# Gated linear attention on one core: the decayed state joins the new k v in PSUM, and VectorE decays it from there

## The chip, the cores and the metric

The kernel runs on one core of a Trainium2 chip. The metric is the device time of one execution in microseconds (us), the median of several; lower is better. The engines are PE (TensorE), DVE (VectorE), ACT (ScalarE), POOL (GpSimd) and SP, whose queue issues most DMAs.

## The reference

Attention with a decaying state, then a soft mixture of experts, then an ELU layer. The change touches the first part alone.

```python
B, H, S, D = 4, 8, 768, 48
state = zeros(B, H, D, D)
for t in range(S):
    state = alpha[:, :, t, :, None] * state + einsum('bhd,bhe->bhde', k[:, :, t], v[:, :, t])
    y[:, :, t] = einsum('bhd,bhde->bhe', q[:, :, t], state)
x = y as (B*S, H*D)
# soft MoE: logits = x @ phi, softmax over tokens and over slots, 8 experts, relu
# then elu(x @ w_in) @ w_out
```

## The kernel before

**Units and chunks.** Tokens come in 24 units of 128 (4 batches of 6), each of two chunks of 64 (g = 0, 1). A tile has the 48 channels of a head in each half of its partitions (h2 = 0, 1, at rows 0 and 64), and four such pairs (j) side by side. Within a chunk the work is matrix products; from chunk to chunk a state of 48 x 48 per head is carried.

**One unit.** `d_sfx` (L421) scans alpha backwards into `sfx`, whose column 0 is the decay over a whole chunk; `d_k` (L426) multiplies k by it in place in the `ring` buffer. `d_ini` (L429, GpSimd) clamps that decay from below; `d_pr` takes its reciprocal (L433) and scans alpha forwards into `pr` (L435). `d_q` (L449) multiplies q by it into `r`, and `d_q2` copies half of `r` (ScalarE, shown as L296, the line of the helper `copy`). `pe_a` (L472) makes the products of k and q, `a_evac` (L478) copies them out, and `mask` (L485, two GpSimd selects) writes their triangle into the other half of `r`. `pe_ktr` (L460) transposes k; `v_move` copies v to other rows. `pe_kv` (L514) makes k v of both chunks in PSUM, in two banks `kv_ps[0]` and `kv_ps[1]`. `pe_y` (L557) multiplies `r` by a tile `vsr` that holds v and, below it, the state, so that one product gives both parts of y; ScalarE copies y to `x`.

**The state.** For each chunk `s_add` (L527, VectorE) adds the decayed state `sp` to k v from PSUM into `sn`; `s_mul` (L537, GpSimd, by `ENG`) multiplies `sn` by the next chunk's decay into `sp`; `s_put` copies `sp` into `vsr` (ScalarE, two copies). At a batch's last chunk nothing is added, and the state in `vsr` is set to zero.

**The order.** `STEP` is an order written by hand: at step s each name is run for unit s - lag, so ("sfx", -2) works on unit s + 2. Steps run from -2 to 23. Each engine takes its instructions in this order. Alongside, one piece of `w_in` per step, in float64, is split into a high and a low part: `conv_a` (L84, L86, L93 on VectorE, L92 on ScalarE) and, a step later, `conv_b` (L659, GpSimd); `loads` fetches the next piece and a part of the expert weights. Every fourth step has work on a group of four units (`post_a`, `post_b`, `post_c`: L579 to L620). The rest of the expert weights is loaded once the attention's buffers are free.

```python
STEP = [("busy0", 0), ("cb", 0), ("kv", 0), ("vc", -1), ("pb", 3), ("sfx", -2), ("ini", -2), ("add0", 0), ("mul0", 0),
        ("busy2", 0), ("a", -1), ("put0", 0), ("k", -2), ("lqka", -1), ("add1", 0), ("mul1", 0), ("pr", -2),
        ("ev", -1), ("put1", 0), ("busy3", 0), ("q", -2), ("ca", 0), ("q2", -2), ("pc", 4), ("loads", 0),
        ("mask", -1), ("pa", 2), ("xtr", 1), ("y", 0), ("check", -2), ("busy1", 0), ("ktr", -2), ("lv", 0)]
```

Of the kernel before, what the change touches and what calls it, by code (L numbers as in the profile page):

```python
# [10 lines left out]
F32 = mybir.dt.float32  # L11
# [43 lines left out]
WPART = 3  # L55
BUSY = (4, 0, 0, 0)

STEP = [("busy0", 0), ("cb", 0), ("kv", 0), ("vc", -1), ("pb", 3), ("sfx", -2), ("ini", -2), ("add0", 0), ("mul0", 0),
# [217 lines left out]
def gla_softmoe_elu_kernel(ctx, tc, qka, vs, vt, phi, w1, w2, w_in, w_out, out):  # L276
    nc = tc.nc
    ctx.enter_context(tc.manual_schedule())
    V, A_, G, T, SY = nc.vector, nc.scalar, nc.gpsimd, nc.tensor, nc.sync
# [122 lines left out]
    st = {}  # L402
# [22 lines left out]
    def d_k(u):  # L425
        eng["k"][0].tensor_mul(split(ks(u)), split(ks(u)), st[u]["sfx"][:, :, 1:])  # L426

    def d_ini(u):
        G.tensor_scalar_max(ini[:, :, 0:1], st[u]["sfx"][:, :, 0:1], DLOW)  # L429

    def d_pr(u):
        a = ring[u % RING][:, 2 * QC:]
        V.reciprocal(ini[:, :, 0:1], ini[:, :, 0:1])  # L433
        pr = wd.tile([128, NP * 2, AW], F32, tag="pr", name="pr")
        V.tensor_tensor_scan(out=flat(pr), data0=a[:, 0:ACOL], data1=flat(ini),  # L435
                             initial=0.0, op0=ALU.mult, op1=ALU.add)
        st[u]["pr"] = pr
# [78 lines left out]

    sp = [None]

    def s_add(u, g):
        if last(u, g):  # L520
            return
        if u % NC == 0 and g == 0:
            sn = wk.tile([128, NP, D], F32, tag="sn", name="sn")
            V.tensor_copy(sn, kv_ps[g])
        else:
            sn = wk.tile([128, NP, D], F32, tag="sn", name="sn")
# [12 lines left out]
    def s_put(u, g):
        if last(u, g):  # L540
# [603 lines left out]
```

## Time and profile before

| | us |
|---|---|
| median of 3 runs | 347.75 (347.74 to 349.73) |
| the profiled execution, its time | 349.67 |
| its span | 347.9 |
| busy: PE, DVE, ACT, POOL | 292.7, 256.1, 206.5, 197.7 |
| steps of the attention, by starts of `pr` | 20.74 to 174.32, 21 steps |

Times in rows are us from the start of the span. A row of a timeline gives the start, the length, the engine, the line, the operation, output and input tiles, shapes, how many instructions are merged, and in brackets how long the engine had been idle and what ended that. Lengths of neighbours on one engine can overlap a little, so what a step costs an engine is read from start to start.

### The profile page before, as it was taken

How to read it: one execution, taken by the hardware profiler on the slowest of the kernel's cores; microseconds unless marked ns; L12 is line 12 of the kernel's file. 1: busy time of each engine (PE TensorE's matmuls, PEld its weight loads, DVE VectorE, ACT ScalarE, POOL GpSimd, SP SyncE). 2: the span in 40 equal slices, each digit the busy share in tenths (PEclk: the TensorE clock that was granted, in tenths of full speed). 3: DMA queues.
4: the chain of work that ended last, by engine and by line, in shares of the span. 5: the costliest groups of instructions: out<-in, count | busy, mean ns of one | idle time of the engine just before them, and what ended most of it. 6: DMA issues, size and time to landing. Idle time of an engine off the chain costs nothing.

```text
span 347.9 us, 9142 instructions
## 1 busy us (share of the span) xinstructions
PE 292.7 (84%) x3632; PEld 214.4 (62%) x3632; DVE 256.1 (74%) x491; ACT 206.5 (59%) x440; POOL 197.7 (57%) x266
## 2 busy tenths in 40 slices
PE   8768688776787676977779899989989999999992
PEld 3766566655566555765656455457767777578881
DVE  5988899998999989999871456189986776176650
ACT  1456676866777677687576223259867657164541
POOL 5476777577577676757753012004689888255450
PEclk9969878999898999699889899999999999999998
DMA  7646887687777777767556889991000000002442
GB/s 287 183 140 218 275 266 255 206 245 260 236 282 210 250 246 253 268 220 219 181 192 259 343 313 424 416 423 61 1 2 0 0 3 0 0 2 110 179 168 96
DMA packets 22049, 66.88 MB, mean 192 GB/s; under 512 B 2416, under 2 KB 8560, under 8 KB 20976
## 3 DMA queue, kind: packets, MB, share of 16 engines
q1 hardware_dynamic: 21296, 63.86, 52.2%
q10 hardware_dynamic: 704, 2.37, 1.8%
q8 instruction: 31, 0.51, 0.6%
q14 instruction: 18, 0.15, 0.1%
HBM read 61.50 MB, written 4.72 MB: 190 GB/s over the span
## 4 chain that ended last, share of the span: by engine, by line
PE 37%; DVE 28%; POOL 15%; ACT 8%; DMA 7%; issue 3%; ACTq 0%; DVEq 0%; SPq 0%; POOLq 0%
PE z_ps L1024 14%; DVE pr L435 8%; POOL wl L659 6%; DMA wo<-w_out 5%; PE hf_ps L996 5%; DVE r L449 4%; PE y_ps L557 4%; POOL ini L429 4%; POOL sp L537 3%; DVE sfx L421 3%; DVE rr L1008 2%; PE h_ps L845 2%; DMA ring<-qka 2%; PE kt_ps L460 2%; DVE sn L527 2%
## 5 line engine op out<-in xcount | busy, mean ns | idle before, releaser
L1024 PE MATMUL z_ps<-rr,wor 128*128 128x512 f32 x288 | 75.8, 395 | 0.8 <-POOL rr L1009 0.8
L557 PE MATMUL y_ps<-vsr,r 128*64 128x64 f32 x768 | 43.8, 250 | 27.3 <-ACT vsr L296 26.6
L1024 PEld LDWEIGHTS z_ps<-rr,wor 128*128 128x128 f32 x288 | 53.5, 188 | 15.4 <-POOL rr L1009 3.4
L1009 POOL TENSOR_TENSOR rr<-mm 128x512 fp32r<-128x512 f32 x36 | 38.6, 1077 | 33.6 <-ACT mm L1002 33.6
L557 PEld LDWEIGHTS y_ps<-vsr,r 128*64 128x64 f32 x768 | 34.5, 156 | 37.4 <-ACT vsr L296 32.5
L485 POOL TENSOR_SCALAR_AFFINE_SELECT r<-at 64x512 f32<-64x512 f32 x48 | 46.5, 969 | 17.4 <-ACT at L478 15.8
L296 ACT COPY vsr<-sp 48x192 f32<-48x192 f32 x88 | 30.8, 350 | 30.7 <-POOL sp L537 29.3
L1002 ACT ACTIVATE mm<-hf_ps 128x1024 f32<-128x1024 f32 x36 | 36.8, 1027 | 15.6 <-PE hf_ps L996 12.5
L659 POOL TENSOR_TENSOR wl<-cva,cvb 128x256 bf16<-128x256 f32 x24 | 30.9, 1289 | 18.5 <-ACT x L296 10.7
L472 PE MATMUL at_ps<-r,ring 64*64 64x64 f32 x768 | 35.3, 235 | 4.5 <-ACT r L296 2.9
L435 DVE TENSOR_TENSOR_SCAN pr<-ring,ini 128x520 f32<-128x520 f32 x24 | 35.7, 1486 | 0.8
L472 PEld LDWEIGHTS at_ps<-r,ring 64*64 64x64 f32 x768 | 30.6, 148 | 7.9 <-ACT r L296 4.7
L1008 DVE SCALAR_TENSOR_TENSOR rr<-hf_ps,mm 128x512 fp32r<-128x512 f32 x36 | 24.8, 688 | 13.3 <-ACT mm L1002 13.0
L996 PE MATMUL hf_ps<-cst,gst 128*128 128x512 f32 x96 | 31.4, 409 | 1.7 <-ACT gst L1078 0.7
L421 DVE TENSOR_TENSOR_SCAN sfx<-ring,imp 128x520 f32<-128x520 f32 x24 | 30.2, 1260 | 2.3 <-DMA ring<-qka 2.3
L537 POOL TENSOR_TENSOR sp<-sn,sfx 128x192 f32<-128x192 f32 x44 | 24.7, 562 | 10.0 <-DVE sn L527 9.9
L296 ACT COPY r<-r 64x512 f32<-64x512 f32 x24 | 14.8, 616 | 19.9 <-DVE r L449 19.6
L527 DVE TENSOR_TENSOR sn<-kv_ps,sp 128x192 f32<-128x192 f32 x40 | 13.8, 346 | 14.4 <-POOL sp L537 11.0
L449 DVE TENSOR_TENSOR r<-ring,pr 128x512 f32<-128x512 f32 x24 | 20.7, 861 | 2.3
L996 PEld LDWEIGHTS hf_ps<-cst,gst 128*128 128x128 f32 x96 | 17.0, 188 | 8.3 <-DVE rr L1008 2.0
L815 POOL COPY c<-chi 128x128 f32<-128x128 f32 x12 | 3.9, 354 | 29.7 <-DVE chi L812 29.7
L429 POOL TENSOR_SCALAR ini<-sfx 128x8 f32<-128x8 f32 x24 | 13.8, 573 | 12.3 <-DVE sfx L421 12.3
(179 smaller groups left out, 596.5 us busy)
## 6 DMA issues: line engine op xcount, KB each, us to landing
ring<-qka SPq DMA_DIRECT2D x22, 772.5 KB, 5.7
w<-w SPq DMA_DIRECT2D x8, 1536.0 KB, 9.7
w<-w SPq DMA_DIRECT2D x21, 512.0 KB, 5.1
raw<-w_in SPq DMA_DIRECT2D x24, 256.0 KB, 2.7
wo<-w_out SPq DMA_DIRECT2D x8, 768.0 KB, 15.5
vsr<-vs SPq DMA_DIRECT2D x48, 96.0 KB, 4.8
out<-wi SPq DMA_DIRECT2D x4, 768.0 KB, 4.0
ring<-qka ACTq DMA_DIRECT2D x2, 772.5 KB, 7.6
```

The costliest lines, as they stand in the source:

```text
L296: (e.copy if e is A_ else e.tensor_copy)(out, in_)
L421: V.tensor_tensor_scan(out=flat(sfx)[:, ::-1], data0=a[:, 1:ACOL + 1][:, ::-1], data1=flat(imp)[:, ::-1], initial=0.0, op0=ALU.mult, op1=A ...
L435: V.tensor_tensor_scan(out=flat(pr), data0=a[:, 0:ACOL], data1=flat(ini), initial=0.0, op0=ALU.mult, op1=ALU.add)
L472: T.matmul(out=at_ps[64 - p0:128 - p0, j, t0:t0 + C], lhsT=k[p0:p0 + 64, j, t0:t0 + C], rhs=r[p0:p0 + 64, h2, j, t0:t0 + C], start=True, s ...
L485: G.affine_select(out=split(r[p0:p0 + 64, h2]), in_=split(at[p0:p0 + 64]), pattern=[[0, 2 * NP], [1, C]], compare_op=ALU.is_ge, fill=0.0, ...
L537: eng[f"mul{g}"][0].tensor_mul(sp[0], sn, pe.to_broadcast([128, NP, D]))
L557: T.matmul(out=y_ps[t0:t0 + C, 2 * j + h2, :], lhsT=r[:, h2, j, t0:t0 + C], rhs=vsr[u % RING][:, h2, g, D * j:D * j + YW], start=True, sto ...
L659: at(s, 2, lambda i: eng["f64b"][0].tensor_mul(wi_lo(i), cva, cvb.bitcast(F32)))
L996: T.matmul(out=h_ps[:, x, :], lhsT=gst[:, 128 * f:128 * f + 128], rhs=cst[:, TG * grp:TG * grp + TG], start=True, stop=True)
L1002: A_.activation(m, hp[p], AF.Relu, scale=-1.0)
L1009: G.tensor_mul(r[1], m[:, 1], m[:, 1])
L1024: T.matmul(out=z_ps[j], lhsT=wo[:, cols], rhs=rs[x], start=(i == 0), stop=(late and i == NFT - 1))
```

## The change

The decayed state is added to the new k v by TensorE: the k v products leave the accumulation open, and two matmuls with the identity as weights (`s_acc`, one for each half of the rows, 192 columns each) add `sp` to the bank. VectorE then multiplies the bank by the decay straight from PSUM into `sp`; `s_add` and the tile `sn` are gone, and no multiplication of the state is on GpSimd. The clamp moves from GpSimd (`d_ini`) to VectorE (in `d_pr`). The y products are made chunk by chunk (`y0`, `y1`) instead of alternating between the chunks, and the copy of y (`x`) is a name of its own. The order of a step is new; `a` stands before the state's work, `k` before it on VectorE, and `y1` and `x` at the end.

```diff
-STEP = [("busy0", 0), ("cb", 0), ("kv", 0), ("vc", -1), ("pb", 3), ("sfx", -2), ("ini", -2), ("add0", 0), ("mul0", 0),
...
+STEP = [("busy0", 0), ("cb", 0), ("kv", 0), ("a", -1), ("acc0", 0), ("vc", -1), ("pb", 3), ("sfx", -2),
+        ("busy2", 0), ("k", -2), ("ev", -1), ("mul0", 0), ("put0", 0), ("lqka", -1), ("mask", -1), ("pr", -2),
+        ("xtr", 1), ("ktr", -2), ("acc1", 0), ("mul1", 0), ("y0", 0), ("put1", 0), ("busy3", 0), ("q", -2), ("ca", 0),
+        ("q2", -2), ("pc", 4), ("loads", 0), ("pa", 2), ("check", -2), ("busy1", 0), ("y1", 0), ("x", 0), ("lv", 0)]
 
-ENG = {'vc0': 'A', 'vc1': 'A', 'mul0': 'G', 'mul1': 'G', 'put': 'AA', ...
+ENG = {'vc0': 'A', 'vc1': 'A', 'mul0': 'V', 'mul1': 'V', 'put': 'AA', ...
-    def d_ini(u):
-        G.tensor_scalar_max(ini[:, :, 0:1], st[u]["sfx"][:, :, 0:1], DLOW)
     def d_pr(u):
         a = ring[u % RING][:, 2 * QC:]
+        V.tensor_scalar_max(ini[:, :, 0:1], st[u]["sfx"][:, :, 0:1], DLOW)
         V.reciprocal(ini[:, :, 0:1], ini[:, :, 0:1])
...
+    def first(u, g):
+        return u % NC == 0 and g == 0
...
-                    T.matmul(out=kv_ps[g][p0:p0 + D, j, :], lhsT=kt[rows, j, p0:p0 + D], rhs=v, start=True, stop=True)
+                    T.matmul(out=kv_ps[g][p0:p0 + D, j, :], lhsT=kt[rows, j, p0:p0 + D], rhs=v, start=(j == 0),
+                             stop=(first(u, g) and j == NP - 1))
...
-    def s_add(u, g):
-        if last(u, g):
+    def s_acc(u, g):
+        if last(u, g) or first(u, g):
             return
-        if u % NC == 0 and g == 0:
...
-            V.tensor_add(sn, kv_ps[g], sp[0])
-        st[u][f"sn{g}"] = sn
+        for h2 in range(2):
+            rows = slice(64 * h2, 64 * h2 + D)
+            T.matmul(out=bank[g][rows, 0:NP * D], lhsT=ident[:, rows], rhs=sp[0].rearrange("p j e -> p (j e)"),
+                     start=False, stop=True)
...
-        eng[f"mul{g}"][0].tensor_mul(sp[0], sn, pe.to_broadcast([128, NP, D]))
+        eng[f"mul{g}"][0].tensor_mul(sp[0], kv_ps[g], pe.to_broadcast([128, NP, D]))
...
-    def pe_y(u):
+    def pe_y(u, g):
...
         for j in range(NP):
             for h2 in range(2):
-                for g in range(2):
-                    t0 = C * g
-                    T.matmul(out=y_ps[t0:t0 + C, 2 * j + h2, :], lhsT=r[:, h2, j, t0:t0 + C],
-                             rhs=vsr[u % RING][:, h2, g, D * j:D * j + YW], start=True, stop=True)
+                t0 = C * g
+                T.matmul(out=st[u]["y_ps"][t0:t0 + C, 2 * j + h2, :], lhsT=r[:, h2, j, t0:t0 + C],
+                         rhs=vsr[u % RING][:, h2, g, D * j:D * j + YW], start=True, stop=True)
+
+    def y_evac(u):
         x = sm.tile([128, DM], F32, tag="x", name="x", bufs=7)
-        copy("x", x.rearrange("p (h e) -> p h e", h=H), y_ps[:, :, 0:D])
+        copy("x", x.rearrange("p (h e) -> p h e", h=H), st[u]["y_ps"][:, :, 0:D])
         st[u] = dict(x=x)
```

## Rows read from the trace of the kernel before

**Rows 1.** Stages: length; busy PE, PEld, DVE, ACT, POOL; clock; DMA share, GB/s

```profile
130.00:180.00 50.00, 38.33 (x741) 30.06 (x742) 44.57 (x76) 35.40 (x90) 35.46 (x50) 0.90 0.66 214
180.00:185.00 5.00, 5.00 (x85) 3.86 (x81) 1.77 (x5) 4.71 (x14) 2.40 (x4) 0.66 0.77 309
205.00:230.00 25.00, 24.29 (x305) 12.69 (x304) 12.93 (x55) 8.02 (x18) 3.29 (x10) 1.00 1.01 419
```

**Rows 2.** Timeline of VectorE, first full step's pr, then one repeating step

```profile
20.74 1.54 DVE L435 TENSOR_TENSOR_SCAN pr<-ring,ini 128x520 f32<-128x520 f32 x1
...
127.17 0.29 DVE L93 TENSOR_SCALAR cvb<-wi 128x256 int32<-128x256 int32 x1
127.38 1.23 DVE L421 TENSOR_TENSOR_SCAN sfx<-ring,imp 128x520 f32<-128x520 f32 x1
...
128.78 0.91 DVE L426 TENSOR_TENSOR ring<-ring,sfx 128x512 f32<-128x512 f32 x1
130.30 0.36 DVE L527 TENSOR_TENSOR sn<-kv_ps,sp 128x192 f32<-128x192 f32 x1 [0.61 <-POOL sp L537]
...
130.80 1.54 DVE L435 TENSOR_TENSOR_SCAN pr<-ring,ini 128x520 f32<-128x520 f32 x1
132.45 0.89 DVE L449 TENSOR_TENSOR r<-ring,pr 128x512 f32<-128x512 f32 x1
133.26 0.74 DVE L84 TENSOR_SCALAR cvb<-raw 128x256 int32<-128x256 int32 x1
...
134.49 0.29 DVE L93 TENSOR_SCALAR cvb<-wi 128x256 int32<-128x256 int32 x1
```

**Rows 3.** Timeline of GpSimd, the same step and an undisturbed mask

```profile
127.62 1.52 POOL L659 TENSOR_TENSOR wl<-cva,cvb 128x256 bf16<-128x256 f32 x1 [0.86 <-ACT x L296]
129.11 0.68 POOL L429 TENSOR_SCALAR ini<-sfx 128x8 f32<-128x8 f32 x1
129.76 0.51 POOL L537 TENSOR_TENSOR sp<-sn,sfx 128x192 f32<-128x192 f32 x1
...
131.76 2.09 POOL L485 TENSOR_SCALAR_AFFINE_SELECT r<-at 64x512 f32<-64x512 f32 x2 [0.51 <-ACT at L478]
...
183.05 1.38 POOL L485 TENSOR_SCALAR_AFFINE_SELECT r<-at 64x512 f32<-64x512 f32 x2 [2.13 <-ACT at L478]
```

**Rows 4.** Timeline of VectorE, a conversion beside little GpSimd work

```profile
180.62 0.45 DVE L84 TENSOR_SCALAR cvb<-raw 128x256 int32<-128x256 int32 x1 [0.29 <-DMA raw<-w_in]
```

**Rows 5.** Instructions of tile pr: ns minimum, median, maximum, first and last start

```profile
L435 DVE TENSOR_TENSOR_SCAN pr<-ring,ini x24: 1241/1541/1545, 9.4 to 174.3; 128x520 f32<-128x520 f32 x24
L449 DVE TENSOR_TENSOR r<-ring,pr x24: 691/887/957, 10.7 to 176.0; 128x512 f32<-128x512 f32 x24
```

**Rows 6.** Timeline of TensorE: the step, then two late stretches

```profile
130.70 1.40 PE L557 MATMUL y_ps<-vsr,r 128*64 128x64 f32 x30 [1.32 <-ACT vsr L296]
132.03 0.66 PE L460 MATMUL kt_ps<-ident,ring 128*128 128x128 f32 x4
...
133.48 0.30 PE L472 MATMUL at_ps<-r,ring 64*64 64x64 f32 x2
134.04 1.14 PE L472 MATMUL at_ps<-r,ring 64*64 64x64 f32 x30 [0.26 <-ACT r L296]
...
181.52 2.60 PE L557 MATMUL y_ps<-vsr,r 128*64 128x64 f32 x32
...
184.54 0.85 PE L618 MATMUL u_ps<-x,le 128*32 128x384 f32 x8
```

**Rows 7.** Timeline of ScalarE, one step

```profile
138.98 0.71 ACT L296 COPY vsr<-sp 48x192 f32<-48x192 f32 x2
139.71 0.44 ACT L92 ACTIVATE cva<-raw 128x256 f32<-128x256 uint32 x1
140.69 0.62 ACT L296 COPY r<-r 64x512 f32<-64x512 f32 x1 [0.54 <-DVE r L449]
```

More of the change, by code (lines that the diff above doesn't have):

```diff
@@ L56 @@
 BUSY = (4, 0, 0, 0)
-STEP = [("busy0", 0), ("cb", 0), ("kv", 0), ("vc", -1), ("pb", 3), ("sfx", -2), ("ini", -2), ("add0", 0), ("mul0", 0),
[3 rows of a table removed]
-ENG = {'vc0': 'A', 'vc1': 'A', 'mul0': 'G', 'mul1': 'G', 'put': 'AA', 'f64b': 'G', 'q2': 'A', 'k': 'V', 'q': 'V', 'kt': 'A', 'x': 'A', 'xt': 'A', 'le': 'A', 'u': 'A', 'lt': 'A'}
+STEP = [("busy0", 0), ("cb", 0), ("kv", 0), ("a", -1), ("acc0", 0), ("vc", -1), ("pb", 3), ("sfx", -2),
[3 rows of a table added]
+ENG = {'vc0': 'A', 'vc1': 'A', 'mul0': 'V', 'mul1': 'V', 'put': 'AA', 'f64b': 'G', 'q2': 'A', 'k': 'V', 'q': 'V', 'kt': 'A', 'x': 'A', 'xt': 'A', 'le': 'A', 'u': 'A', 'lt': 'A'}
 SWDGE = 1024
@@ L513, in pe_kv @@
                     v = vpr[rows, j, :] if g == h2 else vsr[u % RING][rows, h2, g, D * j:D * j + D]
-                    T.matmul(out=kv_ps[g][p0:p0 + D, j, :], lhsT=kt[rows, j, p0:p0 + D], rhs=v, start=True, stop=True)
+                    T.matmul(out=kv_ps[g][p0:p0 + D, j, :], lhsT=kt[rows, j, p0:p0 + D], rhs=v, start=(j == 0),
+                             stop=(first(u, g) and j == NP - 1))
     sp = [None]
-    def s_add(u, g):
-        if last(u, g):
+    def s_acc(u, g):
+        if last(u, g) or first(u, g):
             return
-        if u % NC == 0 and g == 0:
[L523 to L526, printed above, removed]
-            V.tensor_add(sn, kv_ps[g], sp[0])
-        st[u][f"sn{g}"] = sn
+        for h2 in range(2):
+            rows = slice(64 * h2, 64 * h2 + D)
+            T.matmul(out=bank[g][rows, 0:NP * D], lhsT=ident[:, rows], rhs=sp[0].rearrange("p j e -> p (j e)"),
+                     start=False, stop=True)
     def s_mul(u, g):
@@ L532, in s_mul @@
             return
-        sn = st[u].pop(f"sn{g}")
         u2, g2 = (u, 1) if g == 0 else (u + 1, 0)
@@ L548, in s_put @@
             copy("put", s_of(u2, g2, h2), sp[0][rows], h2)
-    def pe_y(u):
+    def pe_y(u, g):
         r = st[u]["r"]
-        y_ps = ps_y.tile([128, H, YW], F32, tag="y", name="y_ps")
+        if g == 0:
+            st[u]["y_ps"] = ps_y.tile([128, H, YW], F32, tag="y", name="y_ps")
         for j in range(NP):
             for h2 in range(2):
-                for g in range(2):
-                    t0 = C * g
-                    T.matmul(out=y_ps[t0:t0 + C, 2 * j + h2, :], lhsT=r[:, h2, j, t0:t0 + C],
-                             rhs=vsr[u % RING][:, h2, g, D * j:D * j + YW], start=True, stop=True)
+                t0 = C * g
+                T.matmul(out=st[u]["y_ps"][t0:t0 + C, 2 * j + h2, :], lhsT=r[:, h2, j, t0:t0 + C],
+                         rhs=vsr[u % RING][:, h2, g, D * j:D * j + YW], start=True, stop=True)
+    def y_evac(u):
         x = sm.tile([128, DM], F32, tag="x", name="x", bufs=7)
-        copy("x", x.rearrange("p (h e) -> p h e", h=H), y_ps[:, :, 0:D])
+        copy("x", x.rearrange("p (h e) -> p h e", h=H), st[u]["y_ps"][:, :, 0:D])
         st[u] = dict(x=x)
@@ L659, in conv_b @@
         at(s, 2, lambda i: eng["f64b"][0].tensor_mul(wi_lo(i), cva, cvb.bitcast(F32)))
-    by_unit = dict(kv=pe_kv, sfx=d_sfx, k=d_k, a=pe_a, ev=a_evac, ini=d_ini, pr=d_pr, q=d_q, q2=d_q2, mask=mask, check=d_check,
-                   y=pe_y, ktr=pe_ktr, vc=v_move, xtr=pe_xtr,
+    by_unit = dict(kv=pe_kv, sfx=d_sfx, k=d_k, a=pe_a, ev=a_evac, pr=d_pr, q=d_q, q2=d_q2, mask=mask, check=d_check,
+                   x=y_evac, ktr=pe_ktr, vc=v_move, xtr=pe_xtr,
                    lqka=lambda u: u + RING < NU and load_qka(u + RING), lv=lambda u: u + RING < NU and load_v(u + RING))
     for g in range(2):
-        by_unit[f"add{g}"] = lambda u, g=g: s_add(u, g)
+        by_unit[f"acc{g}"] = lambda u, g=g: s_acc(u, g)
+        by_unit[f"y{g}"] = lambda u, g=g: pe_y(u, g)
         by_unit[f"mul{g}"] = lambda u, g=g: s_mul(u, g)
```

3 rows, old and new, of the table STEP are left out of this document.

## The prediction

> **What bounds the kernel now.** I read the busy time by stage first, then the timelines of VectorE and GpSimd over one step, then TensorE and ScalarE for room. In the stage of the attention VectorE is the busiest engine, 44.57 of 50 us; TensorE has 38.33, GpSimd 35.46, ScalarE 35.40 [rows 1]. The starts of `pr` for unit 2 and unit 23 are 20.74 and 174.32 [rows 2], 21 steps apart: 7.31 us a step. A plain step repeats from L93 to L93 in 134.49 - 127.17 = 7.32. The steps with group work are longer and those at a batch's end shorter; in the mean they cancel, so I count 21 steps of 7.31.
>
> In that step VectorE has one real wait: 0.61 us ahead of the second `sn`, ended by GpSimd's `sp` [rows 2]. What GpSimd does before it is the loop that sets the step. VectorE's L93 ends at 127.46, GpSimd's `wl` starts at 127.62, then `ini`, then `sp`, which ends at 130.27 [rows 3]; `sn` starts at 130.30 and everything behind it on VectorE, up to the next L93, follows without a gap of any size. (The bracket of `wl` names ScalarE; but it starts 0.16 after the end of L93, which makes its input.) GpSimd is slow in that stretch: `wl` takes 1.52 beside `sfx` and `k`. And VectorE is slow beside GpSimd: `pr` took 1.541 in the median and 1.241 at best, `r` 0.887 and 0.691 [rows 5]; L84 took 0.74 and ended at 134.00, 0.15 after the mask's end at 133.85, and 0.45 where no mask ran [rows 2 to 4].
>
> After the attention the loads of the remaining weights run at 419 GB/s with a DMA share of 1.01 [rows 1]. They start when the attention's buffers come free, so what the attention gains, the end should gain in full; its own traffic is 214 GB/s, and a step that is a twentieth shorter needs little more.
>
> **The change, part by part.** I walk VectorE's new order from the start of `sfx`, start to start, with times of [rows 2] unless named.
>
> `sfx`: 1.23. `k` now comes directly behind it; before, an add from PSUM stood between and `k` started at 1.40. What `k` waits for is GpSimd's `wl`, which ends 1.76 after the start of `sfx` [rows 3] and doesn't move, as it still follows L93. So the end of `k` lies between 1.23 + 0.91 = 2.14 and today's 129.69 - 127.38 = 2.31. I take 2.31: the same wait is in both.
>
> `mul0`, the clamp, the reciprocal: today `sn` and the reciprocal take 0.50 together (130.30 to 130.80). The multiplication has the shape of `sn` and also one operand in PSUM; the clamp is a third small instruction of eight columns, half of the 0.50. Together 0.75, so `pr` starts at 3.06. For `mul0` the trace has no row: its floor is 0.25, its ceiling the 0.51 that GpSimd needs for the same product [rows 3]; `sn` is the nearer row.
>
> `pr`: 1.65 to the next start (130.80 to 132.45), if the mask stands in its way as today; 1.35 if not. `mul1`: 0.25. `q` into `r`: 0.81 (132.45 to 133.26). L84 to L93 is 1.23 now; with the mask out of the way L84 takes 0.45 instead of 0.74 [rows 4], so 0.94. The mask should then be over: it follows `ev`, which follows `a`, and `a` stands near the start of the step. L93 to the next `sfx`: 0.21. Sum: 2.31 + 0.75 + 1.65 + 0.25 + 0.81 + 0.94 + 0.21 = 6.92, against 7.32. The wait of 0.61, the two adds (0.25 each) and 0.29 of L84 go; two multiplications (0.25 each), the clamp (0.25), and 0.25 by which `k` stands longer behind `wl` come.
>
> What GpSimd loses, `ini` (0.68) and two `sp` (0.51 each), is the shortening of the loop; left are `wl`, two mask halves and a small copy, 1.52 + 2.09 + some 0.3, far below a step. GpSimd's queue: the mask goes behind `wl` as before.
>
> TensorE. The two identity matmuls of one `acc` are four matmul records of 192 columns. The nearest row is `u_ps`, eight records of 384 columns in 0.85 [rows 6]; so 0.43 to 0.85 an `acc`. The y products take 1.40 for 30 of 32 records now, with both halves of the array's columns filled in turn; by chunks each half is filled alone, so from 1.40 (if the second chunk runs beside the first) to 2.80. The rest: transpose of k and k v 1.45 (132.03 to 133.48), `a` 1.44 with its wait, the transpose of x some 0.5. Sum 5.65 to 7.9, against 6.92. I take the lower part, as `u_ps` shows that parts of the array work at once (384 columns in 0.11 a record, y's 64 in 0.047). It costs nothing then, under VectorE's cover. But every fourth step has group work, and the granted clock was 0.90 in this stage [rows 1]: part of it lay at the lower of the two levels. A run of y in the stretch with 0.66 took 2.60, not 1.40 [rows 6]. If one step in five is caught so and half a microsecond late at `acc`, that is 0.1 a step. So 7.02.
>
> New waits. `mul0` waits for `acc0`, `mul1` for `acc1`; behind them on VectorE stand the clamp, `pr`, `q`. `acc0` is queued behind `a`, and `a` waits for the copy into `r`, which on ScalarE stands behind `put1` (0.71) and L92 (0.44) [rows 7]. `mul1` starts at 4.71 and ends by 5.07; then 0.71 + 0.44 + 0.62 gives 6.84 for the copy's end, `a` until 6.84 + 1.14 = 7.98, `acc0` until 8.41 to 8.83, and `mul0` is due at 7.02 + 2.31 = 9.33. That holds by 0.5 to 0.9 and costs nothing; a late ScalarE uses it up. `acc1` follows `mul0` at once and has the whole of `pr` as cover. ScalarE itself has 35.40 of 50 us and loses nothing. SP's queue: the next `ring` load still follows `a`, two steps ahead of its use; the load of v follows `y1`, which may end later in the step, but one whole step ahead. Neither bites at the DMA share of 0.66.
>
> Head and tail: the first steps have the same order of sums; behind the last `pr` the work is TensorE's chain of `a`, mask, y. I count no gain and no loss there.
>
> **A rule against it.** L84's row says that an instruction of one SBUF operand stood until the mask was done [rows 2, 3]. The clamp is of that kind, and it now comes about when the mask starts. The Trainium skill, page "SBUF — State Buffer", section "Who interferes with whom", has this as a rule: the port pair shared by VectorE and GpSimd is an exclusive lock held for a whole instruction, and a `tensor_scalar` that can use two ports, or any instruction with two SBUF inputs, blocks or is blocked. By L84's row the trace agrees. What that would give here is the second rival.
>
> **The sum.** 21 steps x (7.31 - 7.02) = 6.1 us. The profiled execution took 349.67 with a span of 347.9, so 343.6 for that one. Its time is 1.9 above the median of the runs, which I take as the base: 347.75 - 6.1 = 341.6.
>
> **The rivals.** First, no change: the loop over ScalarE and TensorE sets the step in place of GpSimd's. From `mul1`: 0.36, `put1` 0.71, L92 0.44, copy 0.62, `a` 1.44 with today's wait, `acc0` 0.85, then from `mul0` to `mul1` 2.40: 6.82, and seven handovers between engines at 0.03 (`sp` to `sn`) to 0.16 (L93 to `wl`): 7.03 to 7.94. At 7.3 the time is 347.5. For it: all of it is in program order. Against it: the dearer ends have to come together, and today's wait in `a` is for that same copy.
>
> Second, slower: the mask moves in front of `pr`. Undisturbed its two halves take 1.38 [rows 3]. My sum has 0.30 (`pr`) and 0.20 (`q`) of it on VectorE. If the clamp waits for the first half and `pr` for the second, up to 1.38 lies there: 6.92 + 0.88 = 7.80, or 347.75 + 21 x 0.49 = 358. It decides from the point where the mask costs VectorE over 0.9. Against it: `mul0`, `mul1` and the reciprocal leave gaps that the mask can use.
>
> Third, slower too: the y products by chunks really take 2.80 and TensorE's 7.9 sets the step: 347.75 + 21 x 0.6 = 360.
>
> Fourth, better: with three instructions fewer on GpSimd nothing is in the way of `pr` and `k`: 6.92 - 0.30 - 0.17 = 6.45, or 329.7.
>
> **How the numbers follow.** My forecast with steps of 6.75 to 7.12 (336 to 343.8): 0.58. First rival 0.22, second 0.10, third 0.04, fourth 0.06. A measurement of this kernel can tell about 1% from no change, 3.5 us. Faster by over 1% (below 344.3): the forecast and the fourth, less a little, 0.62. Within 1%: 0.24. Slower: 0.14. The range from 335 to 350 leaves out the slower rivals and the fourth, about 0.2.
>
> **What would show it.** Right: `pr` to `pr` near 7.0 in plain steps; no idle time ahead of `mul0` and `mul1`; L84 near 0.45; the mask over before `q`. First rival: VectorE idle ahead of `mul0`, ended by TensorE. Second: a long clamp, and `pr` above 1.6. Third: TensorE without idle time and y above 2 us. I am wrong most easily by the lengths of `k`, `pr` and L84, which hang on where GpSimd's mask falls.

## The result, and the profile after

The changed kernel takes 337.63 us in the median of 4 runs (333.61 to 338.95), beside 348.74 for the kernel before (347.74 to 350.21): a ratio of 0.964, interval 0.9536 to 0.9743. Ratios, here and below, leave out runs that are over 1.5% slower than the fastest of the same kernel, here that of 338.95, so they differ a little from the quotients of the medians. The profiled execution took 336.8 with a span of 335.1, so 12.8 us of span are gone. The forecast was faster, 341.6, with a gain of 6.1: the direction and the place were right, the size was half of what came.

Where it went is read from the starts of `pr`. Unit 2's is at 20.54 and unit 23's at 160.64: 6.67 us a step, against 7.31. That is 21 x 0.64 = 13.5 us. From the last `pr` to the start of the last group's softmax (its maximum `mq`, L581) the new kernel needs 0.9 more, and the rest is as long as before (157.8 us in both).

The view of busy time by stage, after: a stretch of the attention, then the loads behind it (length; busy PE, PEld, DVE, ACT, POOL; clock; DMA share, GB/s).

```profile
110.00:160.00 50.00, 45.06 (x885) 36.67 (x885) 48.39 (x91) 41.84 (x104) 29.69 (x32) 1.00 0.77 248
192.00:217.00 25.00, 24.29 (x306) 12.69 (x304) 12.79 (x56) 8.04 (x18) 3.29 (x10) 1.00 1.01 419
```

Beside the rows of before [rows 1], VectorE went from 44.57 to 48.39 of 50 us: it hardly waits any more. TensorE went from 38.33 to 45.06 and the granted clock from 0.90 to 1.00. GpSimd went from 35.46 to 29.69. The loads behind the attention move the same 419 GB/s 13 us earlier, as the forecast had it.

The timeline of VectorE over a plain step, after (its `sfx` starts at 104.71; behind the last line the work of a group follows, at 111.22):

```profile
104.50 0.29 DVE L93 TENSOR_SCALAR cvb<-wi 128x256 int32<-128x256 int32 x1
104.71 1.23 DVE L421 TENSOR_TENSOR_SCAN sfx<-ring,imp 128x520 f32<-128x520 f32 x1
105.98 1.04 DVE L426 TENSOR_TENSOR ring<-ring,sfx 128x512 f32<-128x512 f32 x1
106.94 0.34 DVE L535 TENSOR_TENSOR sp<-kv_ps,sfx 128x192 f32<-128x192 f32 x1
107.20 0.49 DVE L430 TENSOR_SCALAR ini<-sfx 128x8 f32<-128x8 f32 x1
107.72 0.21 DVE L431 RECIPROCAL ini<-ini 128x8 f32<-128x8 f32 x1
107.97 1.50 DVE L433 TENSOR_TENSOR_SCAN pr<-ring,ini 128x520 f32<-128x520 f32 x1
109.39 0.33 DVE L535 TENSOR_TENSOR sp<-kv_ps,sfx 128x192 f32<-128x192 f32 x1
109.64 0.68 DVE L447 TENSOR_TENSOR r<-ring,pr 128x512 f32<-128x512 f32 x1
110.24 0.28 DVE L84 TENSOR_SCALAR cvb<-raw 128x256 int32<-128x256 int32 x1
110.56 0.43 DVE L86 SCALAR_TENSOR_TENSOR wi<-raw,cvb 128x256 int32<-128x256 int32 x1
111.02 0.29 DVE L93 TENSOR_SCALAR cvb<-wi 128x256 int32<-128x256 int32 x1
```

From L93 to L93 that is 6.52, against 7.32 [rows 2]; no row has a wait in brackets. The 0.61 that stood ahead of the second `sn` is gone. In all, VectorE waited 11.0 us for it in the kernel before (from 20 to 180; what waited and for what, us in total, times, longest):

```profile
DVE sn L527 <- POOL sp L537: 11.0, 20, 0.6
```

`q` into `r` (L447) takes 0.68 and L84 0.28, where they took 0.89 and 0.74. The one new thing that is long is the clamp: 0.49 for eight columns.

The timeline of GpSimd over the same step:

```profile
104.94 1.52 POOL L659 TENSOR_TENSOR wl<-cva,cvb 128x256 bf16<-128x256 f32 x1 [1.97 <-DVE cvb L93]
107.00 1.38 POOL L483 TENSOR_SCALAR_AFFINE_SELECT r<-at 64x512 f32<-64x512 f32 x2 [0.54 <-ACT at L476]
108.33 1.16 POOL L440 COPY ends<-sfx 128x32 f32<-128x32 f32 x1
```

The mask (L483) starts at 107.00, just before the clamp, and is over at 108.38; before, it ended 0.15 before L84 did [rows 2, 3]. It takes 1.38, the length that it had undisturbed [rows 3], and now VectorE's clamp and `pr` are what stands. It goes the other way as well: GpSimd's small copy `ends` (L440) is over at 109.49, with `pr` (109.47), and takes 1.16, where it took 0.27 in the step of before (at 133.81).

The waits of the attention, after (engine, tile and line, what it waited for; us in total, times, longest):

```profile
POOL wl L659 <- DVE cvb L93: 21.1, 13, 2.0
...
PE at_ps L470 <- ACT r L296: 12.0, 16, 1.1
...
DVE sp L535 <- PE kv_ps L526: 1.8, 3, 1.3
```

VectorE waits for the new accumulation 3 times, 1.8 us in all. GpSimd waits for VectorE's L93, so it no longer sets the step. TensorE still waits for ScalarE's copy of `r`, as it did before [rows 6].

TensorE's timeline has one accumulation, and behind it the y products of both chunks of a unit, first one chunk, then the other:

```profile
101.13 0.53 PE L526 MATMUL kv_ps<-sp,ident 128*48 128x192 f32 x4
101.49 1.85 PE L555 MATMUL y_ps<-vsr,r 128*64 128x64 f32 x32
```

### The profile page after: what moved, and what is told of

Same layout as the page of the kernel before. It is cut to its first block, busy times and chain, and to the rows that moved or that the text cites. A ratio compares the mean times of both kernels' runs of the same rounds, so it can differ in the third digit from the quotient of the medians.

```text
span 335.1 us, 9452 instructions
## 1 busy us (share of the span) xinstructions
PE 301.2 (90%) x3792; PEld 225.1 (67%) x3792; DVE 251.9 (75%) x515; ACT 209.0 (62%) x440; POOL 168.4 (50%) x198
## 4 chain that ended last, share of the span: by engine, by line
PE 40%; DVE 37%; ACT 10%; issue 9%; DMA 2%; POOL 1%; ACTq 0%; DVEq 0%; POOLq 0%
PE z_ps L1025 14%; DVE sfx L421 6%; PE hf_ps L997 5%; DVE pr L433 4%; PE h_ps L846 4%; DVE r L447 4%; DVE ring L426 3%; PE z_ps L868 3%; DVE sp L535 3%; DVE rr L1009 2%; DVE wi L86 2%; PE y_ps L555 2%; PE at_ps L470 2%; DMA ring<-qka 2%; DVE cvb L84 2%
## 5 line engine op out<-in xcount | busy, mean ns | idle before, releaser
L483 POOL TENSOR_SCALAR_AFFINE_SELECT r<-at 64x512 f32<-64x512 f32 x48 | 40.2, 837 | 29.9 <-ACT at L476 15.7
L555 PEld LDWEIGHTS y_ps<-vsr,r 128*64 128x64 f32 x768 | 47.8, 141 | 6.0 <-issue 3.4
L555 PE MATMUL y_ps<-vsr,r 128*64 128x64 f32 x768 | 50.0, 227 | 0.0
L470 PEld LDWEIGHTS at_ps<-r,ring 64*64 64x64 f32 x768 | 28.3, 134 | 17.5 <-ACT r L296 16.1
L433 DVE TENSOR_TENSOR_SCAN pr<-ring,ini 128x520 f32<-128x520 f32 x24 | 34.1, 1420 | 0.8
L426 DVE TENSOR_TENSOR ring<-ring,sfx 128x512 f32<-128x512 f32 x24 | 23.1, 964 | 0.8
L526 PE MATMUL kv_ps<-sp,ident 128*48 128x192 f32 x160 | 21.3, 344 | 0.0
L440 POOL COPY ends<-sfx 128x32 f32<-128x32 f32 x24 | 19.5, 814 | 3.3 <-DVE sfx L421 3.1
L716 POOL TENSOR_TENSOR wo<-wo,pp 128x384 bf16<-128x384 f32 x16 | 17.3, 1081 | 5.6 <-DVE pp L93 2.8
L458 PE MATMUL kt_ps<-ident,ring 128*128 128x128 f32 x96 | 15.2, 280 | 4.7 <-PE xt_ps L567 2.4
```

The source lines that it names most:

```text
L470: T.matmul(out=at_ps[64 - p0:128 - p0, j, t0:t0 + C], lhsT=k[p0:p0 + 64, j, t0:t0 + C], rhs=r[p0:p0 + 64, h2, j, t0:t0 + C], start=True, s ...
L483: G.affine_select(out=split(r[p0:p0 + 64, h2]), in_=split(at[p0:p0 + 64]), pattern=[[0, 2 * NP], [1, C]], compare_op=ALU.is_ge, fill=0.0, ...
L555: T.matmul(out=st[u]["y_ps"][t0:t0 + C, 2 * j + h2, :], lhsT=r[:, h2, j, t0:t0 + C], rhs=vsr[u % RING][:, h2, g, D * j:D * j + YW], start= ...
```

## The experiments

All ratios are to the kernel before, run on the same chip. The plain step and the mean of 21 steps are read from the starts of `pr` in each profile.

| kernel | us, median (range, runs) | ratio (interval) | plain step | mean step |
|---|---|---|---|---|
| before | 348.74 (347.74 to 350.21, 4) | | 7.32 | 7.31 |
| changed | 337.63 (333.61 to 338.95, 4) | 0.964 (0.9536 to 0.9743) | 6.51 | 6.67 |
| changed, again | 336.67 (334.82 to 340.29, 6) | 0.9653 (0.9591 to 0.9716) | 6.52 | 6.63 |
| 1 adds on VectorE | 354.56 (352.54 to 356.92, 10) | 1.0139 (1.0099 to 1.0179) | 7.44 | 7.42 |
| 2 before, with filler | 350.49 (349.34 to 353.08, 10) | 1.0024 (0.9992 to 1.0057) | 7.33 | 7.32 |
| 3 old order | 338.91 (338.3 to 339.65, 4) | 0.9666 (0.9578 to 0.9754) | 6.53 | 6.83 |
| 4 y alternating | 340.74 (339.12 to 343.68, 4) | 0.9696 (0.9604 to 0.9787) | 6.51 | 6.82 |
| 5 y alternating, filler | 340.34 (337.7 to 341.66, 6) | 0.9712 (0.9649 to 0.9775) | 6.51 | 6.68 |
| 6 clamp against PSUM | 334.47 (333.65 to 336.62, 6) | 0.9572 (0.9517 to 0.9627) | 6.39 | 6.56 |
| 7 clamp on GpSimd | 334.51 (330.16 to 337.13, 6) | 0.9527 (0.9454 to 0.9599) | 6.16 | 6.55 |
| 8 no mask | 332.3 (one run) | | 5.93 | 6.52 |
| 9 clamp on GpSimd, again | 333.4 (331.47 to 335.23, 6) | 0.9562 (0.9523 to 0.96) | 6.16 | 6.48 |
| 10 wl behind the mask | 340.79 (340.09 to 347.75, 6) | 0.9775 (0.9741 to 0.981) | 6.57 | 6.85 |

**The questions.** My theory: the step was set by the loop over GpSimd, the change takes the state off it, and what is left is VectorE's own work, on which the mask lies wherever it falls. The rivals: the gain comes from the new order; or it comes from the clock, which rose from 0.90 to 1.00 in the attention.

**Changed, again** (the same kernel, profiled once more beside runs 5 to 7):

> The changed kernel as it is, beside the next three on one chip. Both theories: 335 to 340 us; a plain step of 6.51.

The ratio came out as 0.9653, the step as 6.52 (plain) and 6.63 (mean).

**1. The adds on VectorE.** The changed kernel, but the sum of k v and decayed state is made by VectorE again, ahead of its multiplication (and the k v products close their accumulation themselves).

```diff
     def s_acc(u, g):
-        if last(u, g) or first(u, g):
-            return
+        return
...
+        old, src = sp[0], kv_ps[g]
+        if not first(u, g):
+            src = wk.tile([128, NP, D], F32, tag="sn", name="sn")
+            V.tensor_add(src, kv_ps[g], old)
-        eng[f"mul{g}"][0].tensor_mul(sp[0], kv_ps[g], pe.to_broadcast([128, NP, D]))
+        V.tensor_mul(sp[0], src, pe.to_broadcast([128, NP, D]))
```

> The changed kernel, but the decayed state is added by VectorE (sn = k v + sp, then sp = sn x decay), not by TensorE; all else as changed. Theory V (VectorE's own row of instructions now sets the step, 6.52 us in a plain step of the changed kernel): two more adds of about 0.25 us start to start each, and two products that now have both operands in SBUF, so a plain step of 7.0 to 7.3 and 347 to 352 us in all, near the kernel before. Theory C (the gain came from TensorE's clock, granted 0.90 to 0.96 before and 1.00 after): TensorE stays nearly as busy, the step stays within 0.1 of 6.52 and the time within 339 to 342.

It is slower than the kernel before, 354.56, and slower than both theories had it: theory V, the nearer one, said 7.0 to 7.3 a plain step and 347 to 352. A stretch of VectorE's timeline:

```profile
71.32 0.34 DVE L536 TENSOR_TENSOR sn<-kv_ps,sp 128x192 f32<-128x192 f32 x1
71.77 0.40 DVE L538 TENSOR_TENSOR sp<-sn,sfx 128x192 f32<-128x192 f32 x1
72.09 0.62 DVE L430 TENSOR_SCALAR ini<-sfx 128x8 f32<-128x8 f32 x1
```

No wait stands here, and VectorE is busy 38.06 of 40 us from 60 to 100. The `sn` takes 0.45 from its start to that of `sp`, which needs its result; two of them make 0.9 a step, where I had put 0.25 for each, and the plain step is 0.93 longer than in the changed kernel. So, with the clamp on VectorE too, taking the multiplication off GpSimd is worth nothing without TensorE's adds, since VectorE is full then. The other half, TensorE's adds with the multiplications left on GpSimd, was not run; that GpSimd's loop set the old step rests on the traces (the 11.0 us of waits that are gone).

**2. The kernel before with more TensorE work.** Three filler matmuls a step at the place `busy2`, to see if the clock alone brings the gain.

```diff
-BUSY = (4, 0, 0, 0)
+BUSY = (4, 0, 3, 0)
```

> The kernel before, with three more identity matmuls (their result is not used) in each step ahead of the products of k and q, to keep TensorE's clock up. Theory V with the loop over GpSimd as the old bound: the granted clock of the attention rises, a plain step stays at 7.32 and the time within 1% of the kernel before, at most 2 us better through the tail. Theory C: the step falls to 6.7 to 7.0 and the time to 338 to 343.

The mean granted clock was 0.951 in the profile, against 0.936, and the step 7.32. That is a weak trial, since the clock rose by so little. Stronger is the trace of before itself, in a row of busy time from 55 to 91:

```profile
55.00:91.00 36.00, 25.94 (x556) 19.88 (x552) 32.56 (x54) 24.47 (x62) 25.62 (x36) 1.00 0.77 248
```

The granted clock was 1.00 there, and the plain steps in it, from the `pr` at 64.92 to that at 86.88, take 7.32 too. So the clock didn't set the old step.

**3. The old order.** The new parts in the order of before: both multiplications around `k`, ahead of the clamp, and the mask late.

```diff
-STEP = [("busy0", 0), ("cb", 0), ("kv", 0), ("a", -1), ("acc0", 0), ("vc", -1), ("pb", 3), ("sfx", -2),
-        ("busy2", 0), ("k", -2), ("ev", -1), ("mul0", 0), ("put0", 0), ("lqka", -1), ("mask", -1), ("pr", -2),
...
+STEP = [("busy0", 0), ("cb", 0), ("kv", 0), ("vc", -1), ("pb", 3), ("sfx", -2), ("acc0", 0), ("mul0", 0),
+        ("busy2", 0), ("a", -1), ("put0", 0), ("k", -2), ("lqka", -1), ("acc1", 0), ("mul1", 0), ("pr", -2),
...
```

> The changed kernel in the order of a step of the kernel before (the sums by TensorE where the adds stood, the two y chunks one behind the other where y stood). Theory V, by which an order matters only where VectorE waits: the second product waits for its sum, which now stands behind the products of k and q on TensorE, about 0.2 us; and GpSimd's mask falls beside the scan and the product of q again, 0.3 to 0.5: plain step 6.6 to 7.0, 338 to 347 us. If the new order alone makes the gain: 7.2 to 7.4 and 346 to 350.

VectorE's timeline, from the clamp to L84:

```profile
67.32 0.16 DVE L430 TENSOR_SCALAR ini<-sfx 128x8 f32<-128x8 f32 x1
67.52 0.21 DVE L431 RECIPROCAL ini<-ini 128x8 f32<-128x8 f32 x1
67.76 1.24 DVE L433 TENSOR_TENSOR_SCAN pr<-ring,ini 128x520 f32<-128x520 f32 x1
69.03 0.96 DVE L447 TENSOR_TENSOR r<-ring,pr 128x512 f32<-128x512 f32 x1
69.91 0.74 DVE L84 TENSOR_SCALAR cvb<-raw 128x256 int32<-128x256 int32 x1
```

and GpSimd's mask beside it:

```profile
67.81 2.69 POOL L483 TENSOR_SCALAR_AFFINE_SELECT r<-at 64x512 f32<-64x512 f32 x2 [1.23 <-ACT at L476]
```

The clamp is short (0.16 for 0.49) and `pr` too (1.24 for 1.50); `q` (0.96 for 0.68) and L84 (0.74 for 0.28) are long instead. The plain step is the same to 0.02. The mask starts 0.05 after `pr`, and here it is the mask that is long (2.69 for 1.38). So the order isn't where the gain comes from: in the main it chooses which instructions pay for the mask. The mean step is 0.16 longer; one step of 8.75 lies in a stretch at 1.2 GHz (139.3 to 146.2). And the end of the attention is 0.65 shorter than in the changed kernel (15.97 for 16.62), which is most of the 0.9 that the new order lost there.

**4. y with the chunks in turn.** Both chunks' products in one run, alternating as before, at the place of `y0`.

```diff
-        ("q2", -2), ("pc", 4), ("loads", 0), ("pa", 2), ("check", -2), ("busy1", 0), ("y1", 0), ("x", 0), ("lv", 0)]
+        ("q2", -2), ("pc", 4), ("loads", 0), ("pa", 2), ("check", -2), ("busy1", 0), ("x", 0), ("lv", 0)]
...
-                t0 = C * g
+                for g in range(2):
+                    t0 = C * g
```

> The changed kernel with the y products of both chunks in one run that alternates between them, at the place of the first chunk. Theory V: TensorE's y falls from about 1.85 to 1.5 us, which VectorE's row hides: plain step 6.52 as before, and 0 to 1 us gained behind the last pr, where TensorE sets the time: 335 to 338. If making y by chunks is part of the gain (y of the second chunk then waits for the state of this step in front of what follows): step 6.7 or more, 341 or more.

The plain step is 6.51 again. The time, 340.74, is above theory V's range and just below the other's. Four stretches at the lower level lie in its steps, where the changed kernel had one, and none when it was profiled again. The busy time around the last of them, where two steps take 7.35 and 7.34 (7.24 and 6.84 in the changed kernel):

```profile
110.00:116.70 6.70, 4.56 (x130) 3.74 (x129) 6.12 (x13) 4.61 (x14) 1.31 (x2) 1.00 0.71 224
116.70:120.10 3.40, 3.40 (x29) 2.88 (x28) 2.21 (x6) 2.74 (x8) 1.60 (x3) 0.50 1.02 361
120.10:126.00 5.90, 5.41 (x135) 4.45 (x133) 5.73 (x11) 5.09 (x12) 3.57 (x5) 1.00 0.69 237
```

In the middle row TensorE, at 1.2 GHz, is busy all 3.40 us, and VectorE only 2.21, as it waits for `kv_ps` twice (0.56 and 0.97). Ahead of it TensorE was busy 4.56 of 6.70 us. Over the 4 runs the mean granted clock was 0.960 to 0.975, in the changed kernel's 4 runs 0.978 to 0.995 (0.976 to 0.993 in the 6 of the repetition). The totals' intervals overlap with the changed kernel's, so the 0.5% between them isn't shown.

**5. The same with filler.** Three filler matmuls a step at `busy1`.

```diff
-BUSY = (4, 0, 0, 0)
+BUSY = (4, 3, 0, 0)
```

> The y products of both chunks in one alternating run, as in the run e4, with three identity matmuls (result not used) in each step behind them, where TensorE waits anyway. In e4 plain steps were as short as in the changed kernel (6.51), but the granted clock fell to the lower level in three stretches of the attention, and the steps there took 7.3 to 8.5. Theory K (y by chunks gains because it keeps TensorE fuller and so its clock up): with the filler the clock stays up, and the time is 335 to 338, no worse than the changed kernel. If the alternating y is dearer by itself (a later wait): 339 to 343, as e4.

From 22.9 to 186.7 the granted clock was 1.00, and the mean step is 6.68, as in the changed kernel: with the clock back, the steps are back. The total isn't: 0.83 more lies in the end of the attention, and two stretches at 1.2 GHz (186.7 to 193.5 and 227.7 to 231.1) behind it. The time of 340.34 lies in the range that I gave for the rival, not for theory K: only the steps bear theory K out.

**6. The clamp against PSUM.** The clamp as a maximum with a constant that lies in PSUM, so that one operand alone comes from SBUF.

```diff
+    low_ps = bank[0][:, 448:456].rearrange("p (j t) -> p j t", t=1)
+    V.memset(low_ps, DLOW)
...
-        V.tensor_scalar_max(ini[:, :, 0:1], st[u]["sfx"][:, :, 0:1], DLOW)
+        V.tensor_tensor(out=ini[:, :, 0:1], in0=st[u]["sfx"][:, :, 0:1], in1=low_ps, op=ALU.max)
```

> The changed kernel with the clamp as a maximum with a constant that lies in PSUM, so that it has one operand in SBUF only and need not wait for the mask; it took 0.49 to 0.52 in a plain step, 0.17 where no mask ran. Theory S (each wait stands by itself): 0.33 less in about 16 of 21 steps, 5 us: 331 to 334. Theory L (VectorE pays for the mask's time on the shared path wherever it falls; the scan behind the clamp, or q, then pays what the clamp saves): 0 to 1.5 us, 335 to 338.

VectorE's timeline:

```profile
66.44 0.15 DVE L432 TENSOR_TENSOR ini<-sfx,kv_ps 128x8 f32<-128x8 f32 x1
66.62 0.20 DVE L433 RECIPROCAL ini<-ini 128x8 f32<-128x8 f32 x1
66.86 1.71 DVE L435 TENSOR_TENSOR_SCAN pr<-ring,ini 128x520 f32<-128x520 f32 x1
```

The clamp is 0.34 shorter, and `pr`, which now meets the mask earlier, 0.21 longer: 0.12 a plain step is kept. (The constant lies in a bank that the trace names `kv_ps`.) Most of the mask's price moved on to the next instruction. The time of 334.47 lies between the two theories' ranges, and the ratio's interval overlaps with the repeated changed kernel's, so this is read from the rows alone.

**7 and 9. The clamp on GpSimd again**, behind `wl`, all else as changed.

```diff
-STEP = [("busy0", 0), ("cb", 0), ("kv", 0), ("a", -1), ("acc0", 0), ("vc", -1), ("pb", 3), ("sfx", -2),
+STEP = [("busy0", 0), ("cb", 0), ("kv", 0), ("a", -1), ("acc0", 0), ("vc", -1), ("pb", 3), ("sfx", -2), ("ini", -2),
...
+    def d_ini(u):
+        G.tensor_scalar_max(ini[:, :, 0:1], st[u]["sfx"][:, :, 0:1], DLOW)
...
-        V.tensor_scalar_max(ini[:, :, 0:1], st[u]["sfx"][:, :, 0:1], DLOW)
```

> The changed kernel with the clamp back on GpSimd, behind the conversion wl and ahead of the mask. If VectorE's own row alone counts: the clamp's 0.5 goes, the reciprocal then waits for GpSimd (wl until 1.76 after the start of sfx, clamp 0.25 to 0.68): between 0.3 better and 0.2 worse a step, 331 to 341. If GpSimd's part of the old loop comes back (L93, wl, clamp, reciprocal, scan): wl ends at 1.76, the clamp behind k at 2.4 to 2.5, so the scan starts no later than now: within 2 us of the changed kernel. Both near; the row of the reciprocal tells them apart by its idle time.

> The changed kernel with the clamp on GpSimd behind wl, a second time. Theory S (the clamp on VectorE is what the change paid too much for): plain steps of 6.16, some 2 to 7 us below the changed kernel's 336.7 to 337.6, a ratio to before of 0.95 to 0.96. If the first run was luck of the chip: a ratio of 0.965.

VectorE's timeline in the second of them, from `mul0` to L84:

```profile
40.46 0.34 DVE L537 TENSOR_TENSOR sp<-kv_ps,sfx 128x192 f32<-128x192 f32 x1
40.72 0.19 DVE L433 RECIPROCAL ini<-ini 128x8 f32<-128x8 f32 x1
40.95 1.50 DVE L435 TENSOR_TENSOR_SCAN pr<-ring,ini 128x520 f32<-128x520 f32 x1
42.38 0.33 DVE L537 TENSOR_TENSOR sp<-kv_ps,sfx 128x192 f32<-128x192 f32 x1
42.62 0.82 DVE L449 TENSOR_TENSOR r<-ring,pr 128x512 f32<-128x512 f32 x1
43.36 0.34 DVE L84 TENSOR_SCALAR cvb<-raw 128x256 int32<-128x256 int32 x1
```

The plain step is 6.16, 0.35 less than in the changed kernel, and no wait for the clamp shows, as GpSimd has it ready (39.95 + 0.68 = 40.63) before the reciprocal starts at 40.72. `mul0` to `pr` takes 0.49 for 1.03; `q` takes 0.14 and L84 0.06 more. So the clamp on VectorE was the part of the change that cost too much. In the mean step 0.15 is left of it against the repeated changed kernel, and the end of the attention is 0.5 longer: 21 x 0.15 - 0.5 = 2.65 us, beside 333.1 - 330.5 = 2.6 in the two spans. (Run 7's mean of 6.55 holds a first step of 8.98, where the granted clock fell.) In the ratios that is at the edge (0.9523 to 0.96 beside 0.9591 to 0.9716); the step alone shows it clearly.

**8. No mask.** ScalarE writes the products of k and q straight into `r`, in two copies, and GpSimd's selects are left out.

```diff
-            G.affine_select(out=split(r[p0:p0 + 64, h2]), in_=split(at[p0:p0 + 64]),
...
+            A_.copy(r[p0:p0 + 64, h2], at_ps[p0:p0 + 64])
```

> The changed kernel without GpSimd's mask: ScalarE writes the products of k and q unmasked into r (so the upper triangle isn't zeroed, and the final test that would send the work to the fallback is held off). If the mask costs VectorE what the rows say (0.33 of the clamp, 0.25 of L84, 0.1 of pr, in all about 0.6 to 0.7 a plain step), the clamp takes about 0.17, L84 about 0.45 to the next start, and a plain step 5.9, as long as no other engine takes over; 21 steps x 0.6 = 13 us less, 323. If TensorE or ScalarE is the next bound, the wait shows ahead of mul0 on VectorE and the step lies between 5.9 and 6.5. If the lengths of VectorE's instructions don't hang on the mask, the step stays at 6.5 and the time at 337.

VectorE's timeline from `mul0` to `pr` of a plain step, and the start of one that waits:

```profile
38.92 0.34 DVE L531 TENSOR_TENSOR sp<-kv_ps,sfx 128x192 f32<-128x192 f32 x1
39.19 0.16 DVE L430 TENSOR_SCALAR ini<-sfx 128x8 f32<-128x8 f32 x1
39.38 0.21 DVE L431 RECIPROCAL ini<-ini 128x8 f32<-128x8 f32 x1
39.62 1.24 DVE L433 TENSOR_TENSOR_SCAN pr<-ring,ini 128x520 f32<-128x520 f32 x1
...
64.28 0.36 DVE L531 TENSOR_TENSOR sp<-kv_ps,sfx 128x192 f32<-128x192 f32 x1 [0.82 <-PE kv_ps L522]
```

Plain steps are 5.93, so the mask costs 0.58 a plain step in the changed kernel: the clamp 0.33 (0.49 - 0.16) and `pr` 0.26 (1.50 - 1.24); `q` and L84 nothing. But the mean step is 6.52, only 0.15 below the changed kernel (0.11 below its repetition), and the time 332.3, where 323 was expected. In steps with group work VectorE waits for the accumulation, up to 1.1 us between 60 and 140, which is behind `a`, which is behind ScalarE's copy of `r`:

```profile
62.55 1.14 PE L470 MATMUL at_ps<-r,ring 64*64 64x64 f32 x30 [1.06 <-ACT r L296]
63.62 0.53 PE L522 MATMUL kv_ps<-sp,ident 128*48 128x192 f32 x4
```

The loop over ScalarE and TensorE is the next bound, close behind VectorE, and in steps with group work it is reached. (ScalarE's copies into `r` are two here instead of one into `at`, so it stands a little nearer than in the changed kernel.)

**10. wl behind the mask.** Run 9 with `cb` moved from the step's start to behind `mask`.

```diff
-STEP = [("busy0", 0), ("cb", 0), ("kv", 0), ("a", -1), ...
+STEP = [("busy0", 0), ("kv", 0), ("a", -1), ...
-        ..., ("mask", -1), ("pr", -2),
+        ..., ("mask", -1), ("cb", 0), ("pr", -2),
```

> The kernel with the clamp on GpSimd, and wl issued behind the mask instead of ahead of it. Theory L (the wait for wl ahead of k is what is left to gain): k comes earlier against sfx, step shorter by up to 0.1 to 0.3, 328 to 334 us. Rival: the mask then stands beside k and the clamp, or the loop over GpSimd closes again, and the step is 6.2 or longer, 335 or more.

The rows of VectorE, and `wl` on GpSimd:

```profile
107.59 0.69 DVE L426 TENSOR_TENSOR ring<-ring,sfx 128x512 f32<-128x512 f32 x1
...
110.63 1.24 POOL L661 TENSOR_TENSOR wl<-cva,cvb 128x256 bf16<-128x256 f32 x1
...
111.90 0.30 DVE L84 TENSOR_SCALAR cvb<-raw 128x256 int32<-128x256 int32 x1 [0.62 <-POOL wl L661]
```

`k` takes 0.69 for 1.04, so 0.35 of `k` was the price of `wl`. But L84 writes the buffer that `wl` reads, and now it waits for it, 16.1 us over the steps. The step is 6.57 plain for run 9's 6.16, and the time 340.79: the rival held, by its loop over GpSimd.

## Why the prediction was right in direction and short in size

**The bound.** "What GpSimd does before it is the loop that sets the step": right. The wait ahead of the multiplication went, and VectorE is full. That the end would keep the whole gain was right as well (157.8 us behind the attention in both).

**The sum, term by term**, predicted and measured in the plain step above:

| start to start | predicted | measured |
|---|---|---|
| `sfx`, `k` | 2.31 | 2.23 |
| `mul0`, clamp, reciprocal | 0.75 | 1.03 |
| `pr` to `mul1` | 1.65 | 1.42 |
| `mul1` | 0.25 | 0.25 |
| `q` to L84 | 0.81 | 0.60 |
| L84 to L93 | 0.94 | 0.78 |
| L93 to `sfx` | 0.21 | 0.21 |
| sum | 6.92 | 6.52 |
| mean over the plain step | 0.10 | 0.15 |

The step that failed is the one that laid the mask on VectorE: "0.30 (`pr`) and 0.20 (`q`)" of it, and so 0.81 for `q`, as before. The same text expected "the mask over before `q`", and then `q` should have been taken at its undisturbed length: rows of 0.691 were there [rows 5]. It measured 0.68. L84 was taken at 0.45, the least disturbed row that I had used [rows 4], and measured 0.28. Those two are 0.37 of the 0.40.

The 0.30 of `pr` was laid to the wrong instruction. In the kernel before, the mask starts at 131.76 [rows 3], 0.96 after `pr`. What stands beside the start of `pr` is GpSimd's second `sp`, and where a batch ends there is none; there its first `sp` is over 0.20 behind the start of `pr` (second line):

```profile
130.74 0.51 POOL L537 TENSOR_TENSOR sp<-sn,sfx 128x192 f32<-128x192 f32 x1 [0.47 <-DVE sn L527]
57.26 1.30 DVE L435 TENSOR_TENSOR_SCAN pr<-ring,ini 128x520 f32<-128x520 f32 x1
```

`pr` takes 1.54 in each of the repeating steps that have this `sp` and 1.29 to 1.30 in the three that don't. In run 3 the mask starts just behind `pr`, and `pr` takes 1.24. So the change took `sp` away from `pr`, and the new order put the mask's second half in its place: 1.50.

From its start to the next, `pr` is short for another reason than I gave. Before, `q` came behind it and needs its result: 1.65 from start to start for a length of 1.54 [rows 2]. Now `mul1` stands behind it, which doesn't need it, and starts 0.08 before the listed end of `pr`. Of the 0.23 by which the term is short, 0.04 is the length and 0.19 the new neighbour. In run 3 `q` stands behind `pr` again and starts 0.03 after its end, not 0.11; by that row the neighbour is worth 0.11. I hadn't seen it in the new order, and no run changes it alone.

Against these stands the clamp, 0.49 instead of 0.25, with 0.28 in its term. It waits for the first half of the mask: it ends at 107.20 + 0.49 = 107.69, which is half of the mask's 1.38 behind the mask's start at 107.00, and it takes 0.16 without a mask (run 8).

**The clock.** I added 0.1 a step for late accumulations at the lower level. The granted clock was 1.00 from 24.3 to 184.7; one stretch at 1.2 GHz, 20.8 to 24.3, lies in one step, which took 8.00 for 6.5, or 0.07 a step over 21. The rest of the 0.15 is steps that aren't plain; the repeated changed kernel had no such stretch in its steps, and its mean is 0.11 over the plain step. The sizes agree nearly, the reason only in part.

**Head and tail.** "No gain and no loss there" was off by 0.9: the last steps are TensorE's chain, and `y1` and `x` now come at the end of it. Run 3 gives back 0.65 with the old order; the other 0.2 stays open.

**TensorE.** The accumulation took 0.53 (bounds 0.43 to 0.85) and y 1.85 (1.40 to 2.80), so the lower part was right; they cost VectorE 1.8 us of waits in all.

**The rivals.** The first (the loop over ScalarE and TensorE) didn't set the step; run 8 shows it close behind, in steps with group work, as soon as VectorE is 0.58 faster. The second (the mask in front of the clamp and `pr`) is what happens, though not enough to turn the sign: the clamp waits for the first half and `pr` for the second, and it costs 0.58, where I put the deciding point at 0.9. The rule of the Trainium skill that I weighed there (page "SBUF — State Buffer", section "Who interferes with whom") fits the clamp: 0.49 beside the mask, 0.16 without one, and 0.15 beside the mask when its second operand lies in PSUM. The third (y by chunks at 2.80) fell at 1.85. The fourth, at 6.45, named a plain step close to the measured one, but not its cause: it had nothing in the way of `pr` and `k`, and both are disturbed (1.50 for 1.24, 1.04 for 0.69).

**Range and size together.** The gain was put at 6.1 us. 21 x (7.31 - 6.67) - 0.9 = 12.5 of the 12.8 us of span; the first counted step starts 0.2 earlier. The time of 337.63 lies in the range from 335 to 350.

## What to carry to other kernels

When an engine leaves a loop, look up what the instructions behind it take undisturbed, in rows of the same trace, and use those lengths wherever the same text says that the disturber will be gone. Look in the timeline of the other engine, too, at what runs when a long instruction starts: that names the disturber, and here it was `sp` and not the mask. Of two instructions of which one needs the other's result, a third that doesn't is worth having between them: here it was worth 0.11 to 0.19 us a step, by rows of two orders. A small instruction put beside another engine's long one can pay for that one's length: leave it on the engine that has the time, as runs 7 and 9 do with the clamp (6.16 for 6.51 a plain step, 0.15 of it left in the mean step of run 9).

## What the runs showed of the hardware

The price of GpSimd's mask on VectorE moves with the order more than it shrinks. It lay on the clamp and `pr` (0.58), on `q` and L84 in run 3 (0.96 for 0.68, 0.74 for 0.28: 0.74 in all, in a step of 6.53, as `k` pays less for `wl` there, 0.90 for 1.04), and on `pr` in run 6 (1.71 for 1.24: 0.47). `pr` grows by 0.15 less than it overlaps with the GpSimd instruction that started first: by 0.30 where `sp` ends 0.45 after its start (before), by 0.26 where the mask ends 0.41 after it (changed), by 0.47 where the mask ends 0.62 after it (run 6: 65.94 + 1.54 against 66.86). These are three places, not a rule for others. Only when the whole of the mask was gone (run 8), or when an instruction that paid was itself gone (runs 7 and 9), did the step get much shorter.

The granted clock of a kernel differs from run to run, and the time follows: 333.61 us at a mean of 0.995 and 338.46 at 0.979, for the same changed kernel. The y products by chunks take TensorE longer (1.85; with the chunks in turn 1.40 before, and 1.10 to 1.57 in run 4), and the clock stayed at 2.4 GHz in nearly all of the steps; with the chunks in turn it fell three times more, and with filler added it stayed up again (run 5). But y by chunks alone doesn't keep the clock up: run 1 makes it by chunks too. The busy time from 20 to 160 in run 1, then in the changed kernel:

```profile
20.00:160.00 140.00, 115.84 (x2045) 98.37 (x2045) 133.32 (x255) 99.12 (x244) 68.78 (x82) 0.90 0.72 237
20.00:160.00 140.00, 125.29 (x2404) 103.14 (x2403) 134.32 (x246) 109.78 (x269) 81.98 (x91) 0.99 0.80 257
```

In run 1 the granted clock was 0.90 there, as in the kernel before (0.89), for 0.99 in the changed kernel. A trial that changes nothing but TensorE's busy time in the changed kernel was not made, so what kept the clock up stays open.
